# Moving one block's short convolution from VectorE to TensorE in a fused attention and long-convolution kernel

## The chip, the core and the metric

The kernel runs on one core of one Trainium2 chip. A core has five engines that run their own instruction streams and wait for one another through semaphores: TensorE (PE in the profile, with its weight loads as PEld), VectorE (DVE), ScalarE (ACT), GpSimd (POOL) and SyncE (SP), and 16 DMA engines that serve queues issued from SP, ACT and POOL. The metric is device time in microseconds (us); three runs of the kernel before gave 206.75, 206.83 and 206.92 us.

## What is computed

Two independent parts share the launch, and their outputs stand side by side in the result (2048 rows of 1152 bf16 values).

```python
# A: sliding, dilated local attention. S=2048, D=576, 32 heads of 18, window 8, dilation 2
qkv = x @ wqkv
logits[s, w] = q[s] . k[s - 2*w] * 18**-0.5        # -1e9 where s - 2*w < 0
o = softmax(logits over w) weighted sum of v[s - 2*w]
a = o @ wo

# B: gated long convolution, one channel at a time (D=576)
k_shift[t] = sum over j=0..3 of k[t - j] * shift_k[:, j]     # four taps per channel
kv = k_shift * v
y  = causal convolution of kv with ssm_k over 2048 steps, by a transform of length 4096
b  = q * (y + kv * ssm_D)
```

## The kernel before

**Tiling.** Sequence rows are cut into four blocks of 512. Part A projects q, k and v so that channels lie on the 128 partitions (jobs `q..`, `k..`, `v..`, for instance `k13a` and `k13b`, by `project`), multiplies shifted k by q on VectorE (`L..`, `pair_product`), sums over the 18 channels of a head on TensorE (`G..`, `pair_sum`), takes the softmax in four steps `sm0a` to `sm0d` for one half of the positions and `sm1a` to `sm1d` for the other, spreads the weights over partitions by DMA (`D0` to `D5`), weighs v on VectorE (`V..`), sums on TensorE (`A..`) and multiplies by `wo` (`O..`). Part B forms kv for block i by the four taps (`Ti`), folds it into a symmetric and an antisymmetric half (`Mi0`, `Mi1`), transforms it by cosine and sine tables on TensorE (`x..`), does the same with the filter (`F`, `K..`), multiplies spectra on VectorE (`p..`), sums them on TensorE (`z..`), goes back (`i..`, `b..`) and gates with q (`g..`).

**Order.** Nothing is scheduled by a compiler. The string `ORDER` lists the jobs; each one, when called, issues its instructions to every engine that it uses, and every engine runs its instructions in that order. A prime behind a job's name sets a variant inside it. `LHOMES`, `VHOMES`, `OHOMES` and `PHOMES` say which buffer a job's result goes to, so a job also waits until an older job has read that buffer. PSUM holds four slots of two banks; a job that multiplies on TensorE takes one or two (`banks`) and whoever empties it gives it back.

**Taps.** `taps(i)` (lines 511 to 536) runs on VectorE alone. `load_k` loads the block seven rows deep into `kj`, positions on partitions, so that a tap is a shift inside a partition; `skb` holds the tap weights on every partition, which `spread_taps` makes at the start. For blocks 1 to 3 there are two multiplications of 4608 elements for each partition (line 517), three additions of 2304 (line 520) and the multiplication with v (line 536). `mirror` then turns kv into its two halves with the constant `fold`.

**ScalarE's tables.** The sine tables are made early (line 382, job `S1` last). Job `Ex` (`exponential`, lines 658 to 660) then loads the table set that holds both the exponential and the logarithm; the softmax uses Exp at line 752, Ln at line 763 and Exp at line 764.

Of the kernel before, what the change touches and what calls it, by code (L numbers as in the profile page):

```python
# [17 lines left out]
PSUM = bass.MemoryType.PSUM  # L18

ORDER = """  # L20
    T0 k03a' T1 S1 k03b I1 k02a k02b Lk2 Lv2 I0 k00a' Lk3 Lv3 M01 X5 k00b q10a Ex q10b Lf3 T2 Lo3 q13a' q13b
    k10a k10b T3 k13a' Lf2 k13b q12a q12b N2 Lo2 k01a M10 k01b Lf1 M00 k11a k11b q11a M11 q11b Lf0 N3 Lw SV L001
    k12a M20 k12b x001 M21 x021 q24a x020 q24b x000 Lo1 k24a Fr Lo0 Z2 N1 RG3 k24b RG2 F3 RG0 F2 L000 K310 G000
    K311 K210 K211 L002 K313 G001 RG4 F1 G002 L003 G003 K302 L004 G004 K301 L010 K212 L011 K303 K213 K203 N0 F0
    L012 K200 K300 G010 L013 K201 K312 K202 RG1 G011 G012 K113 K103 G013 L014 G014 K112 K102 K101 L100 K100 K010
    K111 K110 sm0a K001 K013 sm0b v24a' L101 v24b L102 G100 L103 G101 K012 sm0c sm0d U3 U2 K000 K011 K003 G102
    K002 D0 D1 v11a v11b G103 L104 G104 ak00 M30 v12a' v12b ak02 v01a ak01 L110 G110 M31 L111 G111 v01b v00a'
    L112 G112 L113 Wl v00b G113 x031 U1 L114 G114 V04 v10a' v10b A04 sm1a sm1b v02a v02b v03a' sm1c v03b x201
    V10 V11 sm1d V12 A10 v13a' v13b D2 x330 x310 x301 V13 A11 V20 V21 x200 x331 x230 x010 x221 A20 x321 V22 x210
    x011 V23 D3 V34 ax02 x220 x030 x300 D4 A21 V40 V41 A34 D5 O000' x211 V42 x320 x231 x111 x131 Tx2 A40 V43  # L30
    x120 x101 ax00 x130 ax01 V50 x121 x311 O001 A41 V51 O100' p000 x100 x110 O010 A50 V52 z000 O011' V53 O101
    A51 Tk2 p010 z010 ax10 O020' O021 p020 z020 O110' ak10 i000 p200 i02880 Q0 p100 z100 p101 p110 p111 Q1 z101
    i02881 i001 p121 p120 O111 z110 p201 z111 z120 p210 z121 O120 p211 z200 z210 z211 p212 z212 z201 p202 z202
    Tx3 p220 Tk3 p221 O030' p222 O121 b0288 z220 p301 z221 O031' p302 b00 z222 p303 i200 i100 g0 Q2 p300 y300
    p312 i12880 i201 i101 i12881 z300 z301 z303 p310 p311 y310 O130 b10 b1288 p313 g1 Q3 p322 O131' z310 p320
    z311 p321 z313 i22880 i300 b20 y320 p323 i22881 i301 b2288 g2 z320 z321 z323 b30 i3384L g30 g3384
"""

LHOMES = (0, 1, 2, 0, 1, 2, 0, 1, 2, 0, 1, 2, 0, 1, 0, 1, 0, 1, 0, 1)
# [12 lines left out]
def kernel(  # L52
# [13 lines left out]
    nc = tc.nc  # L66
    Bsz, S, D = A_x.shape
# [6 lines left out]
    kf = B_k.flatten_outer_dims()  # L74
    vf = B_v.flatten_outer_dims()
# [14 lines left out]
    NBL, BL = 4, 512  # L90
# [3 lines left out]
    HD = 288  # L94
    HB = 4 * D
# [25 lines left out]
    def kv_of(i):  # L121
        return view(xw, HB * KVS[i], [[D, 4], [1, D]])
# [21 lines left out]
    sp1 = s1.enter_context(tc.tile_pool(name="s1", bufs=1, reuse_waits="tile"))  # L144
# [23 lines left out]
    Ks = main.tile([128, 12 * HB], BF16, name="Ks")  # L168
# [8 lines left out]
    kjs, vts = [], []  # L177
# [6 lines left out]
    def load_k(i):  # L184

        eng = nc.sync
        kj = sp1.tile([128, 7, D], BF16, name="kj", bufs=2)
        r0 = BL * i
        low = [(0, 64)]
        if i == 0:  # L190
            nc.gpsimd.memset(kj[0:1, 0:3, :], 0.0)
            nc.gpsimd.dma_start(kj[0:1, 3:7, :], kf[0:4, :].unsqueeze(0))
            low = [(1, 49), (49, 64)]
        for a, b in ((3, 7), (0, 3)) if i == 0 else ((0, 7),):
            for p0, p1 in low:
# [5 lines left out]
        kjs.append(kj)  # L201

    def load_v(i):
        vt = sp1.tile([128, 4, D], BF16, name="vt", bufs=2)
# [3 lines left out]
        vts.append(vt)  # L208

    def load_filter(m):  # L210

# [14 lines left out]
    ident = main.tile([128, 128], BF16, name="ident")  # L226
# [22 lines left out]
    flip = main.tile([128, 128], BF16, name="flip")  # L249
# [58 lines left out]
    def halves(ap):  # L308
        return ap.rearrange("p (h d) -> p h d", h=2)
# [197 lines left out]
    for n in range(2):  # L507
        job(f"I{n}", table_i, n)
    tt = nc.vector.tensor_tensor

    def taps(i):
# [23 lines left out]
            add(pair[1])  # L535
        tt(kv, kv, vt, ALU.mult)
# [599 lines left out]
```

## Time and profile before

| what | value |
|---|---|
| median of 3 runs | 206.83 us (206.75 to 206.92) |
| profiled execution, first to last instruction | 204.6 us, granted TensorE clock 0.994 |
| PE busy | 196.9 us (96%), 2074 matmuls |
| DVE busy | 192.3 us (94%), 146 instructions |
| ACT busy | 155.6 us (76%) |
| POOL busy | 60.8 us (30%) |
| DMA | 38.48 MB, mean 188 GB/s |

The profile states the execution's span of 204.6 us and no separate time for what lies around it; the median is 2.2 us above that span. A row that begins with a line number (L322) speaks of that line of the kernel. An arrow in a name points from what is read to what is written (`ps_proj<-xw`); the releaser behind a wait is the engine and line whose end ended it. The chain of work that ended last follows the program back from its last instruction, at each step to what released it. A matmul's record includes its way through the array, so records overlap, and the start of one to the start of the next says more than a record's length.

### The profile page before, as it was taken

Reading aid. Unit: us, or ns where it says so; the run is one execution under the profiler, and the core shown is the slowest. Engines: PE = TensorE matmul, PEld = TensorE weight load, DVE = VectorE, ACT = ScalarE, POOL = GpSimd, SP = SyncE. Lnnn points to the kernel's source line nnn. Section 1 sums busy time; section 2 is a strip of 40 time slices with the busy share of each in tenths; the row PEclk is TensorE's granted clock in tenths of the full one; section 3 lists DMA queues with packets and bytes.
Section 4 is the critical chain, followed back from the end, with each engine's and each line's share of the span. In section 5 each row is a group of like instructions: output and inputs, shape, how many; then the busy total and the mean of one; then the engine's idle time right before and its main releaser. Section 6 shows DMA issues by size and latency. Waiting matters only on the chain.

```text
span 204.6 us, 5004 instructions
## 1 busy us (share of the span) xinstructions
PE 196.9 (96%) x2074; PEld 109.9 (54%) x2074; DVE 192.3 (94%) x146; ACT 155.6 (76%) x223; POOL 60.8 (30%) x106
## 2 busy tenths in 40 slices
PE   7999999999989999999999999999999999999990
PEld 2543544334455646543245556776666767766660
DVE  7559999999999999999999999999999999899992
ACT  4788995678899999966578678886778767767760
POOL 8989500011348581400380000004090001030300
PEclk9999999999999999999999999999999999999997
DMA  6999899989509869999899990879989303944555
GB/s 197 280 293 306 175 289 373 214 177 281 169 3 146 111 82 185 167 180 222 157 235 216 248 244 34 141 183 334 186 227 233 100 28 122 227 130 145 153 182 150
DMA packets 34916, 38.48 MB, mean 188 GB/s; under 512 B 17523, under 2 KB 28911, under 8 KB 34894
## 3 DMA queue, kind: packets, MB, share of 16 engines
q1 hardware_dynamic: 26668, 24.29, 46.5%
q0 software_dynamic: 5760, 11.36, 29.5%
q10 hardware_dynamic: 2466, 2.51, 3.6%
q8 instruction: 16, 0.26, 0.5%
q14 instruction: 6, 0.05, 0.1%
HBM read 13.11 MB, written 4.72 MB: 87 GB/s over the span
## 4 chain that ended last, share of the span: by engine, by line
PE 88%; DMA 3%; ACT 2%; DVE 2%; issue 1%; SPq 1%; DVEq 0%
PE ps_proj L322 18%; PE ps_fx L682 8%; PE ps_wo L888 8%; PE ps_z L975 8%; PE ps_inv L1010 7%; PE ps_acc L824 7%; PE ps_fk L567 5%; PE ps_log L720 5%; DMA Ks<-in_A_x_dram 3%; PE ps_proj L333 3%; PE ps_proj L326 3%; PE ps_proj L439 3%; PE ps_fk L568 3%; PE ps_fold L545 2%; PE ps_wo L880 1%
## 5 line engine op out<-in xcount | busy, mean ns | idle before, releaser
L322 PE MATMUL ps_proj<-xw 128*128 128x512 bf16 x160 | 38.5, 380 | 0.0
L706 DVE TENSOR_TENSOR av<-qk 128x4096 bf16<-128x4096 bf16 (+1 forms) x16 | 31.7, 2014 | 0.1
L322 PEld LDWEIGHTS <-xw 128*128 128x128 bf16 x160 | 13.9, 98 | 19.4 <-issue 5.7
L988 ACT ACTIVATE av<-ps_z 128x768 bf16<-128x768 f32 x23 | 17.2, 811 | 6.5 <-PE ps_z L975 6.0
L517 DVE TENSOR_TENSOR tB<-kj,skb 128x4608 bf16<-128x4608 bf16 (+1 forms) x8 | 19.3, 2416 | 0.1
L950 DVE TENSOR_TENSOR qk<-xw,Ks 128x2304 bf16<-128x2304 bf16 x14 | 18.9, 1354 | 0.3 <-PE ps_z L975 0.3
L684 ACT ACTIVATE xw<-ps_fx 128x576 bf16<-128x576 f32 x32 | 18.6, 665 | 0.3 <-PE ps_fx L682 0.2
L618 ACT ACTIVATE Ks<-ps_fk 128x576 bf16<-128x576 f32 x32 | 18.6, 699 | 0.2 <-PE ps_fk L568 0.2
L355 ACT ACTIVATE qk<-ps_proj 128x1024 bf16<-128x1024 f32 x14 | 14.3, 1023 | 5.2 <-PE ps_proj L333 2.8
L888 PE MATMUL ps_wo<-qk 128*128 128x288 bf16 x128 | 17.9, 287 | 0.0
L626 POOL DMA_DIRECT2D Ks<-Ks x8 | 10.1, 1426 | 26.0 <-PE ps_back L1059 19.3
L682 PE MATMUL ps_fx<-xw,TB 128*128 128x288 bf16 x128 | 17.7, 287 | 0.0
L567 PE MATMUL ps_fk<-Ks,TB 128*128 128x384 bf16 x62 | 16.5, 327 | 0.1
L824 PE MATMUL ps_acc<-av,ident 64*64 64x512 bf16 x160 | 15.3, 378 | 0.0
L1010 PE MATMUL ps_inv<-av,TI 128*128 128x288 bf16 (+1 forms) x112 | 15.2, 292 | 0.0
L568 PE MATMUL ps_fk<-Ks,TB 128*128 128x192 bf16 x62 | 15.2, 246 | 0.0
L682 PEld LDWEIGHTS <-TB 128*128 128x128 bf16 x128 | 11.9, 98 | 5.9 <-issue 2.7
L888 PEld LDWEIGHTS <-qk 128*128 128x128 bf16 x128 | 11.7, 98 | 5.4 <-issue 2.7
L355 ACT ACTIVATE v<-ps_proj 128x1024 bf16<-128x1024 f32 x9 | 9.3, 1033 | 6.5 <-PE ps_proj L322 4.5
L813 DVE TENSOR_TENSOR av<-Ks,v 128x4096 bf16<-128x4096 bf16 x6 | 13.5, 2286 | 0.0
L827 ACT ACTIVATE qk<-ps_acc 128x1024 bf16<-128x1024 f32 x8 | 8.2, 1024 | 6.7 <-PE ps_acc L824 6.7
L1010 PEld LDWEIGHTS <-TI 128*128 128x128 bf16 x112 | 10.6, 98 | 4.2 <-issue 1.1
(195 smaller groups left out, 441.6 us busy)
## 6 DMA issues: line engine op xcount, KB each, us to landing
Ks<-Ks POOLq DMA_DIRECT2D x8, 576.0 KB, 7.8
TB<-av SPq DMA_DIRECT2D x12, 256.0 KB, 5.4
kj<-in_B_k_dram SPq DMA_DIRECT2D x6, 504.0 KB, 7.0
vt<-in_B_v_dram SPq DMA_DIRECT2D x8, 288.0 KB, 5.3
Ks<-av SPq DMA_DIRECT2D x8, 256.0 KB, 5.6
out_dram<-qk ACTq DMA_DIRECT2D x5, 288.0 KB, 3.7
Ks<-in_A_x_dram SPq DMA_DIRECT2D x2, 576.0 KB, 5.4
xw<-in_A_wqkv_dram SPq DMA_DIRECT2D x2, 576.0 KB, 6.2
```

The source lines that it names most:

```text
L322: nc.tensor.matmul(ps[:, jp, :], wq(kb, comp, 128 * ct, 128), xT(kb, 1024 * jj + 512 * jp, 512), **se)
L355: nc.scalar.activation(view(t, o + pad + 1024 * jj, [[512, 2], [1, 512]]), ps[:], ACT.Copy)
L517: tt(to, view(kj, row * D, [[D, n], [D, 4], [1, D]]), view(skb, row * D, [[D, n], [0, 4], [1, D]]), ALU.mult)
L567: nc.tensor.matmul(o[:, 0:2], w, rhs[:, 0:2], start=start, stop=stop)
L568: nc.tensor.matmul(o[:, 2], w, rhs[:, 2], start=start, stop=stop)
L618: nc.scalar.activation(view(Ks, k_at(m, cs ^ (m & 1)) + 96 * gi, [[768, 3], [384, 2], [1, 96]]), acc3(ps), ACT.Copy, scale=(PSG, MSG)[cs][ ...
L682: nc.tensor.matmul(ps[:, pm, 0:HD], TX[:, 2 * pm + c, 128 * gi:128 * gi + 128], kv[:, 2 * c + pm, HD * h:HD * h + HD], start=(c == 0), sto ...
L706: tt(view(P, at, [[step, 4], [256, nj], [1, 256]]), view(t, o + 256 * hh, [[0, 4], [512, nj], [1, 256]]), view(tk, ok + 2 + 8 * ug + 256 * ...
L824: nc.tensor.matmul(acc[64 * o:64 * o + 64, h, :], ident[64 * h:64 * h + 64, 64 * h:64 * h + 64], view(P[s], 256 * u, [[2048, 2], [1, 256]] ...
L888: nc.tensor.matmul(ps[:, r, 0:HD], oT(hh, j + 2 * r, t)[:, o:o + 128], wo[:, t // 2, t % 2, HD * h:HD * h + HD], start=(t == 0 and not fli ...
L950: tt(product_home(n), view(xw, HB * XG[i] + QTR * t, [[HB, 3], [1, QTR]]), view(Ks, k_at(j - i, 0) + QTR * t, [[HB, 3], [1, QTR]]), ALU.mult)
L1010: nc.tensor.matmul(ps[:, c, 0:n], TI[:, sl, pm, 128 * c:128 * c + 128], Yall(j % 2, pm, sl, slice(c0, c0 + n)), start=(pm == 0 and sl == 0 ...
```

## The change

Block 3, the fourth, no longer has its taps taken by VectorE. Its rows of k are loaded channel by channel with two transposing DMAs into space at the start of `Ks` (528 positions, 16 of them ahead of the block). For each 128 channels and each tap there is a 128 by 128 diagonal matrix with the tap's weights, 16 of them and four of 64 by 64 for the last 64 channels; VectorE makes them with two multiplications of `ident` by the weights, which two DMAs on ScalarE's queue bring in at the start as `taps_w`. On TensorE, 64 positions of transposed k (every fourth column) are the weights and the diagonal is the moving operand; four taps add up in PSUM, even and odd partition halves side by side. That makes three jobs: `T31` and `T30` with 64 matmuls each, and `T3t` with 32. VectorE multiplies each result by v, straight out of PSUM. Block 3's v is loaded to the place of kv, with the two halves on the lower and upper 64 partitions rather than interleaved, and `mirror` uses a second constant `fold_t` for it, made by GpSimd. Blocks 0 to 2 are as before.

The whole `ORDER` is new. VectorE's share of block 3, ahead of the first products of pairs (L590 is a small negation, L706 a product), before:

```order
L536 TENSOR_TENSOR xw<-xw,vt 128x2304
L517 TENSOR_TENSOR tB<-kj,skb 128x4608
L520 TENSOR_TENSOR xw<-tB 128x2304
L517 TENSOR_TENSOR tB<-kj,skb 128x4608
L520 TENSOR_TENSOR xw<-xw,tB 128x2304 x2
L536 TENSOR_TENSOR xw<-xw,vt 128x2304
L590 TENSOR_SCALAR Ks<-Ks 1x576 x2
L706 TENSOR_TENSOR av<-qk 128x4096
```

The same place on VectorE in the changed kernel, where L765 is the product of pairs, L578 and L589 the multiplication by v out of PSUM:

```order
L563 TENSOR_TENSOR xw<-xw,vt 128x2304
L765 TENSOR_TENSOR av<-qk 128x4096
L649 TENSOR_SCALAR Ks<-Ks 1x576 x2
L765 TENSOR_TENSOR av<-qk 128x4096
L765 TENSOR_TENSOR v<-qk 128x4x1024
L765 TENSOR_TENSOR av<-qk 128x4096
L765 TENSOR_TENSOR av<-qk 128x2048
L578 TENSOR_TENSOR xw<-ps_tap,xw 128x2x512
L765 TENSOR_TENSOR v<-qk 128x4x1024
L578 TENSOR_TENSOR xw<-ps_tap,xw 128x2x512
L589 TENSOR_TENSOR xw<-ps_tap,xw 128x4x64
L765 TENSOR_TENSOR av<-qk 128x4096
```

The six instructions of block 3's taps are gone, the products of pairs follow block 2 at once, and three multiplications out of PSUM stand among them.

Job `Ex` moved from behind `q10a` to the very end of `ORDER`. ScalarE around the first softmax, before (L752 is the exponential, L763 and L764 the logarithm and the exponential of the sum, L618 and L355 evictions of the filter's transform and of v's projection):

```order
L618 ACTIVATE Ks<-ps_fk 128x6x96 x9
L752 ACTIVATE av<-av 128x2048
L355 ACTIVATE v<-ps_proj 128x1024
L618 ACTIVATE Ks<-ps_fk 128x6x96
L763 ACTIVATE av<-ps_tot 128x256
L764 ACTIVATE av<-av 128x256
L618 ACTIVATE Ks<-ps_fk 128x6x96 x4
```

and in the changed kernel, where L811, L822 and L823 are those three and L677 and L377 those evictions:

```order
L677 ACTIVATE Ks<-ps_fk 128x6x96 x2
L811 ACT_TABLE_LOAD
L811 ACTIVATE av<-av 128x2048
L677 ACTIVATE Ks<-ps_fk 128x6x96
L377 ACTIVATE v<-ps_proj 128x1024
L822 ACT_TABLE_LOAD
L822 ACTIVATE av<-ps_tot 128x256
L823 ACT_TABLE_LOAD
L823 ACTIVATE av<-av 128x256
L677 ACTIVATE Ks<-ps_fk 128x6x96 x3
```

Three table loads stand inside the first softmax now; the second has two, ahead of its logarithm and ahead of its last exponential, and one more stands at the program's end with `Ex`. The one that stood at line 659 among the projections is gone.

The diff, cut to its core (the rest of `ORDER` is new in the same way):

```diff
 ORDER = """
-    T0 k03a' T1 S1 k03b I1 k02a k02b Lk2 Lv2 I0 k00a' Lk3 Lv3 M01 X5 k00b q10a Ex q10b Lf3 T2 Lo3 q13a' q13b
-    k10a k10b T3 k13a' Lf2 k13b q12a q12b N2 Lo2 k01a M10 k01b Lf1 M00 k11a k11b q11a M11 q11b Lf0 N3 Lw SV L001
...
+    k00a' T0 k01a k01b T1 k00b Lk2 k03a' M01 k02a X5 Lv2 k02b I0 k10a S1 Lw T2 q10a k10b SV q10b k24a k24b k11a
+    RG0 L000 Lf2 k03b N2 q11a Lf3 Lk3 k13a' N3 Lo2 k11b Lv3 Lf0 k13b Lo3 q11b M00 k12a k12b M11 q12a q12b RG3
+    L001 RG2 q13a' F3 q24a q24b Lf1 L002 q13b M21 G000 G001 Fr Lo0 L003 L004 RG4 Lo1 F2 T31 G002 G003 G004 RG1
+    L010 T30 T3t K313 L011 K311 M30 v03a' v03b K210 L012 N1 K312 G010 G011 K302 K300 K212 K203 N0 L013 L014 K202
...
+    z310 z311 z313 Q3 O131' p320 i300 b20 O121 y320 z320 p321 i301 p323 g2 z321 z323 b30 i3384L g30 g3384 Ex
 """
@@
+    taps_w = main.tile([128, 5, 4], BF16, name="taps_w")
+    nc.scalar.dma_start(taps_w[:, 0:4, :], B_shift_k[0:512, :].rearrange("(kb p) j -> p kb j", p=128))
+    nc.scalar.dma_start(taps_w[64:128, 4, :], B_shift_k[512:576, :])
@@
+        if i in TURNED:
+            t = view(Ks, 0, [[1, 5 * KT]]) if i == TURNED[0] else sp1.tile([128, 7, D], BF16, name="kj", bufs=2)
+            rows = kf[BL * i - 16:BL * i + BL]
+            eng.dma_start_transpose(view(t, 0, [[KT, 4], [1, KT]]), rows[:, 0:512])
+            eng.dma_start_transpose(view(t, 4 * KT, [[1, KT]]), rows[:, 448:576])
+            kjs[i] = t
+            return
@@
+    nc.vector.tensor_tensor(diag, ident[:].unsqueeze(1).unsqueeze(1).to_broadcast([128, 4, 4, 128]),
+                            taps_w[:, 0:4, :].unsqueeze(3).to_broadcast([128, 4, 4, 128]), ALU.mult)
+    nc.vector.tensor_tensor(diag_t, ident[64:128, 64:128].unsqueeze(1).to_broadcast([64, 4, 64]),
+                            taps_w[64:128, 4, :].unsqueeze(2).to_broadcast([64, 4, 64]), ALU.mult)
@@
+    def turned(i, kb, c, j, e):
+        return view(kjs[i], KT * kb + 16 + (259 - c if e else c) - j, [[4, 64]])
+
+    def taps_pe(i, h):
+        ps, slot = banks("ps_tap")
+        for c in range(2):
+            for kb in range(4):
+                for j in (3, 2, 1, 0):
+                    for e in range(2):
+                        nc.tensor.matmul(ps[64 * e:64 * e + 64, c, 128 * kb:128 * kb + 128],
+                                         turned(i, kb, 2 * h + c, j, e), diag[:, kb, j, :],
+                                         start=(j == 3), stop=(j == 0), tile_position=(0, 64 * e))
+        kv = kv_of(i)[:, 2 * h:2 * h + 2, 0:512]
+        tt(kv, ps[:], kv, ALU.mult)
+        slots.append(slot)
+
+    def taps_pe_tail(i):
+        ps, slot = banks("ps_tap")
+        for c in range(4):
+            for j in (3, 2, 1, 0):
+                for e in range(2):
+                    nc.tensor.matmul(ps[64 * e:64 * e + 64, 0, 64 * c:64 * c + 64], turned(i, 4, c, j, e)[64:128],
+                                     diag_t[:, j, :], start=(j == 3), stop=(j == 0), tile_position=(64, 64 * e))
+        kv = kv_of(i)[:, :, 512:576]
+        tt(kv, view(ps, 0, [[64, 4], [1, 64]]), kv, ALU.mult)
+        slots.append(slot)
```

More of the change, by code (lines that the diff above doesn't have):

```diff
@@ L26 @@
[L26 to L35, printed above, removed]
@@ L36 @@
-    z311 p321 z313 i22880 i300 b20 y320 p323 i22881 i301 b2288 g2 z320 z321 z323 b30 i3384L g30 g3384
+    k00a' T0 k01a k01b T1 k00b Lk2 k03a' M01 k02a X5 Lv2 k02b I0 k10a S1 Lw T2 q10a k10b SV q10b k24a k24b k11a
+    RG0 L000 Lf2 k03b N2 q11a Lf3 Lk3 k13a' N3 Lo2 k11b Lv3 Lf0 k13b Lo3 q11b M00 k12a k12b M11 q12a q12b RG3
+    L001 RG2 q13a' F3 q24a q24b Lf1 L002 q13b M21 G000 G001 Fr Lo0 L003 L004 RG4 Lo1 F2 T31 G002 G003 G004 RG1
+    L010 T30 T3t K313 L011 K311 M30 v03a' v03b K210 L012 N1 K312 G010 G011 K302 K300 K212 K203 N0 L013 L014 K202
@@ new lines @@
+    K310 G012 F1 L100 G013 G014 F0 K200 v00a' K201 K303 v00b G100 K211 K301 L101 sm0a sm0b G101 L102 K213 v02a
+    Z2 v02b L103 sm0c G102 L104 sm0d D1 K102 K003 G103 L110 K001 G104 K111 v01a L111 U3 K101 K113 K011 v01b G110
+    K002 K000 G111 K100 K110 K012 L112 K013 L113 G112 K112 L114 K010 K103 G113 v11a G114 D0 V11 V10 v11b M20
+    ak00 v24a' v24b sm1a M31 x010 A10 sm1b v10a' v10b V13 v12a' sm1c D2 x231 x200 x210 V04 sm1d ak01 A04 x230
+    v12b V12 x211 x221 x030 V20 D3 A11 v13a' v13b V21 x000 D4 x201 A20 x330 x311 x220 V22 V23 V34 Wl x020 M10
@@ new lines @@
+    ax00 A21 x310 Tx2 x321 ak02 A34 V41 x320 V40 O000' x011 x031 V42 x001 x021 ax02 x121 ax01 x110 A40 V43 D5
+    x101 x131 I1 O001 x120 O100' p000 A41 V50 x100 V51 x301 U2 x111 U1 Tk2 x130 V52 O101 A50 x331 z000 O110' V53
+    A51 p010 z010 x300 O010 ax10 p020 z020 p101 O111 O011' p111 i02880 Q0 i000 ak10 p100 z100 Tx3 p110 p120 z101
+    i02881 i001 z120 p121 z121 z110 z111 O020' p200 p210 p211 z200 p212 z210 z211 z212 Tk3 p201 i100 z201 p202
+    z202 i101 p222 b00 i12880 p220 p221 z220 p301 b0288 g0 z221 p302 z222 i12881 b10 p303 O030' i22880 b1288
@@ L37 @@
+    i200 i22881 O031' p300 O021 y300 p312 z300 z301 b2288 z303 Q1 g1 i201 p311 Q2 p310 y310 O120 p313 O130 p322
+    z310 z311 z313 Q3 O131' p320 i300 b20 O121 y320 z320 p321 i301 p323 g2 z321 z323 b30 i3384L g30 g3384 Ex
 """
@@ L176, in kTok @@
         return view(Ks, k_at(m, 2), [[D, 4], [1, D]])
-    kjs, vts = [], []
+    kjs, vts = {}, {}
+    TURNED = (3,)
+    KT = 16 + BL
+    diag = view(Ks, 3 * HB, [[512, 4], [128, 4], [1, 128]])
+    diag_t = view(Ks, 3 * HB + 2048, [[64, 4], [1, 64]])[64:128]
     def load_x(qtr):
@@ L200, in load_k @@
                                                     ap=[[4 * D, 64], [-D, b - a], [1, D]]))
-        kjs.append(kj)
+        kjs[i] = kj
     def load_v(i):
+        if i in TURNED:
+            nc.sync.dma_start(kv_of(i)[0:64], vf[BL * i:BL * i + 256, :].rearrange("(p c) d -> p c d", c=4))
+            nc.sync.dma_start(kv_of(i)[64:128], bass.AP(tensor=vf.tensor, offset=vf.offset + (BL * i + 256 + 3) * D,
+                                                        ap=[[4 * D, 64], [-D, 4], [1, D]]))
+            return
         vt = sp1.tile([128, 4, D], BF16, name="vt", bufs=2)
@@ L207, in load_v @@
                                               ap=[[4 * D, 64], [-D, 4], [1, D]]))
-        vts.append(vt)
+        vts[i] = vt
     def load_filter(m):
@@ L266 @@
                                 base=-127, channel_multiplier=1)
+    fold_t = main.tile([128, 128], BF16, name="fold_t")
+    for h in range(2):
+        nc.gpsimd.tensor_tensor(fold_t[:, 64 * h:64 * h + 64], ident[:, 0:64], flip[:, 0:64], (ALU.add, ALU.subtract)[h])
     flip2 = main.tile([128, 128], BF16, name="flip2")
@@ L544, in mirror @@
                 for e in range(2):
-                    nc.tensor.matmul(pss[pm][64 * e:64 * e + 64, h, 0:HD], fold[:, 64 * pm:64 * pm + 64],
+                    nc.tensor.matmul(pss[pm][64 * e:64 * e + 64, h, 0:HD], (fold_t if i in TURNED else fold)[:, 64 * pm:64 * pm + 64],
                                      kv[:, 2 * n + e, HD * h:HD * h + HD], start=True, stop=True, tile_position=(0, 64 * e))
@@ L551 @@
     for i in range(NBL):
-        job(f"T{i}", taps, i)
+        if i in TURNED:
+            for h in range(2):
+                job(f"T{i}{h}", taps_pe, i, h)
+            job(f"T{i}t", taps_pe_tail, i)
+        else:
+            job(f"T{i}", taps, i)
         for n in range(2):
```

3 lines of the change are left out of this document (removed).

## The prediction, made before the changed kernel ran

> **What bounds the kernel now.** I read the page's engine totals and its chain first.
>
> ```profile
> span 204.6 us, 5004 instructions
> PE 196.9 (96%) x2074; PEld 109.9 (54%) x2074; DVE 192.3 (94%) x146; ACT 155.6 (76%) x223; POOL 60.8 (30%) x106
> PE 88%; DMA 3%; ACT 2%; DVE 2%; issue 1%; SPq 1%; DVEq 0%
> ```
>
> TensorE and VectorE are both nearly always busy, but the chain that ended last runs through TensorE for 88% of the span and through VectorE for 2%. Busy TensorE records need not mean full speed, so the next view is the windows: TensorE from its wait for the second quarter of x (9.87) to its last matmul (199.9).
>
> ```profile
> 9.87:56.00 46.13, 46.13 (x315) 19.56 (x316) 42.91 (x28) 37.50 (x48) 16.11 (x38) 1.00 1.01 254
> 56.00:62.00 6.00, 5.25 (x44) 3.43 (x43) 6.00 (x4) 5.99 (x9) 2.97 (x5) 1.00 0.13 19
> 62.00:82.00 20.00, 20.00 (x195) 11.63 (x195) 19.86 (x16) 19.95 (x35) 12.18 (x13) 1.00 0.89 131
> 82.00:100.00 18.00, 18.00 (x159) 7.80 (x156) 18.00 (x12) 13.39 (x19) 2.30 (x2) 1.00 0.95 190
> 100.00:150.00 50.00, 50.00 (x596) 30.06 (x598) 49.74 (x31) 37.45 (x55) 9.84 (x13) 1.00 0.85 197
> 150.00:199.90 49.90, 49.23 (x736) 33.77 (x727) 47.96 (x39) 35.78 (x54) 8.83 (x12) 1.00 0.57 154
> ```
>
> The columns are the window, its length, then busy time of PE, PEld, DVE, ACT and POOL. TensorE lacks 0.75 us between 56 and 62 and 0.67 us in the last window, 1.4 us of 190. Its list of waits says the same, and VectorE's largest wait is its first data.
>
> ```profile
> PE ps_log L720 <- DVE av L706: 0.6, 1, 0.6
> PE ps_inv L1029 <- ACT av L988: 0.3, 1, 0.3
> PE ps_back L1038 <- ACT v L1031: 0.2, 1, 0.2
> PE ps_x L410 <- DMA Ks<-in_A_x_dram: 0.2, 1, 0.2
> PE ps_z L975 <- DVE Ks L950: 0.2, 1, 0.2
> DVE xw L517 <- DMA kj<-in_B_k_dram: 4.2, 1, 4.2
> 12.28 1.36 DVE L517 TENSOR_TENSOR xw<-kj,skb 128x2304 bf16<-128x2304 bf16 x1 [4.16 <-DMA kj<-in_B_k_dram]
> ```
>
> Then the pace of runs in the chain, to see whether "busy" hides waiting:
>
> ```profile
> 20.42 0.57 PE ps_ti L397 x16
> 25.62 0.25 PE ps_x L428 x8
> 29.10 3.56 PE ps_proj L322 x16
> 85.03 0.87 PE ps_tot L762 x8
> ```
>
> L322 moves 512 columns: 3.56/16 = 222 ns each, 2.3 columns in a ns. L762 moves 256: 109 ns each, 2.35 in a ns. Two different jobs, one of them amid ScalarE's and VectorE's busiest time, go at one pace for a column, so TensorE streams; it does not dawdle behind others. VectorE is full as well (42.91 + 6.00 + 19.86 + 18.00 + 49.74 + 47.96 = 184.5 of 190, and 2.4 of the missing 5.5 lie ahead of its first data at 12.28). The two are balanced, so work taken off VectorE gains no more than the waits for it, while work put on TensorE lengthens the kernel.
>
> **The change part by part.** *VectorE's taps of block 3 go.* Their rows:
>
> ```profile
> 44.36 2.55 DVE L517 TENSOR_TENSOR tB<-kj,skb 128x4608 bf16<-128x4608 bf16 x1
> 46.94 1.36 DVE L520 TENSOR_TENSOR xw<-tB 128x2304 bf16<-128x2304 bf16 x1
> 48.34 2.56 DVE L517 TENSOR_TENSOR tB<-kj,skb 128x4608 bf16<-128x4608 bf16 x1
> 50.93 2.75 DVE L520 TENSOR_TENSOR xw<-xw,tB 128x2304 bf16<-128x2304 bf16 x2
> 53.71 1.36 DVE L536 TENSOR_TENSOR xw<-xw,vt 128x2304 bf16<-128x2304 bf16 x1
> L1020 DVE TENSOR_TENSOR TB<-ps_back,TB 128x384 bf16<-128x384 f32 x2 | 1.0, 554 | 0.6 <-PE ps_back L1038 0.6
> L1020 DVE TENSOR_TENSOR TB<-ps_back,TB 128x768 bf16<-128x768 f32 x1 | 1.0, 954 | 0.0
> ```
>
> They sum to 10.6 us. Back come two multiplications of 1024 elements out of PSUM and one of 256. From 554 and 954 ns for 384 and 768 such elements, one element costs 1.04 ns, so 1024 take 1.22 and 256 take 0.42: 2.9 us. VectorE is relieved of 7.7 us.
>
> *The diagonals*, 2048 elements on 128 partitions and 256 on 64, both factors in SBUF, one repeated along the inner dimension. Low end: the softmax's subtraction, which also repeats an operand, takes 1.2 us for 2048 (L748, below). High end: the PSUM pace, about 2.3. With the small one, 1.4 to 2.7 us. VectorE waits 4.2 us for the first `kj` just there; that covers either, so I charge nothing. Without that cover it would be VectorE's time, not TensorE's.
>
> *TensorE's taps.* 128 matmuls of 64 weight columns by 128 moving ones, alternating between the array's column halves, each with its own weight load, and 32 by 64. No job of TensorE is dropped. The nearest row is L397: the same shape, the same alternation, own weights each: 0.57/16 = 36 ns. A floor comes from L762's pace: 128 columns take 54 ns, and with two halves at once 27 ns each. So the 128 cost 3.5 to 4.6 us. For the 32 the nearest row is L428 (same 64 wide weights, twice the moving columns), 31 ns: 1.0 at most, 0.5 at half. Together 4.0 to 5.6; long runs pay the change between jobs seldom, so I take 4.6.
>
> The Trainium skill, "TensorE: Matmul & The Clock Gate", section "Back-to-back issue gap", speaks against this change: it gives about 81 ns for each matmul in a stream of weight load and 128-column matmul. By it the 160 would cost an estimated 13.0 us; the trace's 36 ns for L397, which is such a stream, disagrees, and the sum keeps the row.
>
> *The start.* `taps_w` is 576 pieces of 8 bytes in two DMAs ahead of the first table load on ScalarE, while the second quarter of x, for which TensorE waits, is on its way.
>
> ```profile
> 3.12 6.70 DMA Ks<-in_A_x_dram
> q10 hardware_dynamic: 2466, 2.51, 3.6%
> ```
>
> ScalarE's queue shows 3.6% of 16 engines' 204.6 us for 2466 packets, 48 ns each at a kilobyte; 36 pieces on each engine are then at most 1.7 us, and zero if they slip between. Tiny pieces should cost well under a kilobyte's: 0.3.
>
> *Queues.* On SP, block 3's two transposing loads stand behind two of the four filter loads. Their data are wanted only at `T31`, some 50 us into the program, so nothing waits. The early `SV` job only lets the products start earlier.
>
> *Waits filled.* Of the five TensorE waits above, those for L706 (0.6) and L950 (0.2) should go when VectorE is ahead, and the 0.2 at other hand-overs: minus 1.0 at most, and I take all of it. The two ScalarE ones lie in the last job, which is unchanged.
>
> *New waits.* `M30` follows `T3t` on TensorE after two filter units only, and needs VectorE's two multiplications: 1.22 + 0.42 against about 1 us of cover: 0.3 with the semaphores. Bigger: with `Ex` at the end, ScalarE loads tables inside the softmaxes, three times in the first and twice between the second's sum and its result.
>
> ```profile
> L659 ACT ACT_TABLE_LOAD x1 | 1.3, 1283 | 0.0
> 86.36 0.42 ACT L764 ACTIVATE av<-av 128x256 bf16<-128x256 f32 x1
> 87.64 1.22 DVE L756 TENSOR_TENSOR av<-av 128x2048 bf16<-128x2048 bf16 x1
> L748 DVE TENSOR_TENSOR av<-av 128x2048 bf16<-128x2048 bf16 x1 | 1.2, 1225 | 0.0
> 108.58 2.28 DVE L813 TENSOR_TENSOR qk<-Ks,v 128x4096 bf16<-128x4096 bf16 x1
> 110.37 0.42 ACT L764 ACTIVATE xw<-xw 128x256 bf16<-128x256 f32 x1
> 110.82 1.23 DVE L756 TENSOR_TENSOR av<-av,xw 128x2048 bf16<-128x2048 bf16 x1
> ```
>
> VectorE's scaling L756 followed ScalarE's last exponential by 0.9 us in the first softmax and by nothing in the second. Three loads of 1.28 are 3.85, less 0.9: 3.0 late; two are 2.5 late. VectorE waits some 5.5 us of its 7.7, and behind L756 stand the next products of pairs and of v. For those TensorE's `G` and `A` jobs wait. Nothing arrives if VectorE is that far ahead, 5.5 if TensorE is right behind; VectorE is ahead by part of its relief, so I take 1.0. The load taken out at line 659 was not on the chain.
>
> The Trainium skill, "ScalarE: Activation LUTs", section "What ACT_TABLE_LOAD costs", adds about 1380 ns of draining to the 1283 of a load. By it the first softmax would be 7.1 us late and the second 5.3; here the single row shows no idle time ahead of the load (0.0), and what a load between two dependent activations costs no run here shows.
>
> **Sum.** On the profiled execution: 204.6 + 4.6 + 0.3 - 1.0 + 0.3 + 1.0 = 209.8 us of span. The 2.2 us between its span and the median of 206.83 stay, so the forecast is 206.83 + 5.2 = **212.0 us**. Its own bounds: +3.0 (cheap taps, no new waits) to +8, 209.8 to 214.8.
>
> **Rivals.**
> 1. *VectorE sets the end, and the kernel gets faster.* Place: the whole stretch from 12 us on. For it: VectorE hardly waits there, and TensorE's ends are modelled. It would save 7.7 less up to 5.5 lost at the softmaxes, 199.1 to 204.6, about 202. It decides only if TensorE's 190 us hide at least the 4.6 of the taps as waiting; against it stands the one pace of L322 and L762.
> 2. *Strided weights load slowly.* The taps' weight columns are four positions apart, L397's adjacent. The only strided read of this kind in the trace is ScalarE's regrouping L780, 1316 ns for 576 elements at a step of 9, against 665 for L684, which reads adjacent ones from PSUM. Twice the price for the taps: +4.6, 216.6 us.
>
> ```profile
> L780 ACT ACTIVATE xw<-Ks 128x576 bf16<-128x576 bf16 x5 | 6.6, 1316 | 0.0
> L684 ACT ACTIVATE xw<-ps_fx 128x576 bf16<-128x576 f32 x32 | 18.6, 665 | 0.3 <-PE ps_fx L682 0.2
> ```
>
> 3. *The softmax waits reach TensorE whole*: 5.5 instead of 1.0, 216.5 us. For it: TensorE follows VectorE closely (0.2 us waits for L950, none long).
> 4. *Weight loads one at a time*: one of 64 columns is recorded as 109 ns; 160 of them are 17.4, 12.8 above my 4.6: 224.8 us. L397 itself ran at 36 ns a matmul, hence hardly likely.
>
> ```profile
> L397 PEld LDWEIGHTS <-TB 128*64 128x64 bf16 x32 | 1.0, 109 | 0.7 <-issue 0.7
> ```
>
> 5. *The new order sheds more than it adds*: shorter changes between TensorE's jobs and no new waits, 206.5 to 209. The only named waits are 1.5 us, less than the cheapest taps, so this needs gains that no row shows.
>
> **How the numbers follow.** Forecast 69%, rival 3 10%, rival 2 8%, rival 5 6%, rival 1 5%, rival 4 2%. The range 209.0 to 215.8 holds the forecast and the milder half of rivals 2 and 3. What a measurement can tell from no change is about 0.2%, 0.4 us. Faster: rival 1 and no more, 5%. The same: half of rival 5, 3%. Slower: 92%.
>
> **What would show it.** Right: `ps_tap` runs of 64 matmuls in 1.8 to 2.3 us; TensorE busy in all windows from 10 us on and ending 4 to 6 us later; VectorE with waits of 2 to 3 us at both scalings, released by ScalarE, and others for `ps_tap`. Rival 2 shows as `ps_tap` runs of 4 us, rival 3 as TensorE waits for pair products or for v's. I am wrong if TensorE's last matmul ends before 201 us, which would mean that its records were elastic.

## Result and the profile after

The changed kernel takes **219.18 us** (218.04 to 219.81), the kernel before 206.88 beside it: ratio 1.060, 95% interval 1.056 to 1.064, 12.3 us slower. The forecast was 212.0 with a range up to 215.8: the sign is right, the size is not. The profiled execution has a span of 218.1 us. Its engine totals and the shares of its chain:

```profile
span 218.1 us, 5322 instructions
...
PE 205.7 (94%) x2221; PEld 114.7 (53%) x2234; DVE 188.7 (87%) x145; ACT 162.7 (75%) x228; POOL 78.3 (36%) x108
...
PE 86%; ACT 9%; issue 2%; DVE 1%; ACTq 0%; DVEq 0%
```

TensorE still sets the end, but ScalarE now has 9% of the chain where it had 2%. TensorE's last matmul started at 199.61 us before and starts at 213.24 now; the rest of the program behind it is as long as before. So all of the loss lies ahead of that matmul. Windows of the changed kernel (window, length, busy time of PE, PEld, DVE, ACT and POOL with the number of instructions, then the granted clock, the DMA share and GB/s):

```profile
80.00:92.00 12.00, 10.01 (x82) 4.85 (x82) 7.79 (x5) 11.79 (x15) 3.35 (x5) 1.00 0.76 131
...
108.00:123.00 15.00, 12.72 (x117) 7.46 (x118) 10.16 (x7) 12.61 (x17) 0.00 (x0) 0.89 0.63 128
```

The two softmaxes (80 to 92 and 108 to 123) stand out: TensorE lacks 2.0 and 2.3 us there, VectorE 4.2 and 4.8. ScalarE is full in the first (11.79 of 12.00) and busy for 12.61 of 15.00 in the second, where the clock was lowered too. TensorE's waits in the changed kernel (waiting tile and line, releaser, us in total, times, longest):

```profile
PE ps_acc L897 <- ACT xw L743: 1.6, 1, 1.6
...
PE ps_fk L626 <- ACT Ks L677: 1.1, 1, 1.1
...
PE ps_tot L821 <- ACT av L811: 0.8, 1, 0.8
PE ps_inv L1069 <- ACT av L1047: 0.6, 1, 0.6
...
PE ps_fx L741 <- ACT xw L822: 0.3, 1, 0.3
```

and VectorE's, which waits for both scalings (L815) as forecast:

```profile
DVE av L815 <- ACT xw L823: 2.7, 1, 2.7
...
DVE av L815 <- ACT av L823: 2.2, 1, 2.2
```

Four of these five TensorE waits (1.6 + 1.1 + 0.8 + 0.3 = 3.8 us) are in the softmaxes, and all are for ScalarE, none for VectorE's products. L677 and L743 are evictions of PSUM that have nothing to do with the softmax, and L822 empties the slot of the softmax's own sum. L821 is that sum on TensorE: it waits for the exponential itself (L811), which a load put off. ScalarE's instructions around the first softmax say why they are late (start, duration, line):

```profile
81.52 1.28 ACT L811 ACT_TABLE_LOAD   x1
82.81 1.91 ACT L811 ACTIVATE av<-av 128x2048 bf16<-128x2048 bf16 x1
84.63 0.63 ACT L677 ACTIVATE Ks<-ps_fk 128x576 bf16<-128x576 f32 x1
85.16 1.02 ACT L377 ACTIVATE v<-ps_proj 128x1024 bf16<-128x1024 f32 x1
86.19 1.28 ACT L822 ACT_TABLE_LOAD   x1
87.49 0.38 ACT L822 ACTIVATE av<-ps_tot 128x256 f32<-128x256 f32 x1
87.89 1.28 ACT L823 ACT_TABLE_LOAD   x1
89.19 0.42 ACT L823 ACTIVATE av<-av 128x256 bf16<-128x256 f32 x1
89.51 1.71 ACT L677 ACTIVATE Ks<-ps_fk 128x576 bf16<-128x576 f32 x3
```

ScalarE takes its instructions in order. From 86.19 to 89.51 it empties one slot only, that of the sum (L822): two loads and two short activations stand ahead, and three evictions then run one after another. TensorE has four PSUM slots and runs out of them (start, duration, and in brackets the wait and its releaser):

```profile
90.19 0.32 PE L626 MATMUL ps_fk<-Ks,TB 128*128 128x384 bf16 x1 [1.06 <-ACT Ks L677]
```

The Trainium skill, "ScalarE: Activation LUTs", section "What ACT_TABLE_LOAD costs", adds some 1380 ns of draining to a load. The trace disagrees for the load between L822 and L823, which needs L822's result: L822 ends at 87.49 + 0.38 = 87.87, the load starts at 87.89 and ends at 89.17, and L823 starts at 89.19.

The taps, from the chain of the changed kernel:

```profile
56.13 2.12 PE ps_tap L574 x64
...
59.66 2.13 PE ps_tap L574 x63
61.79 1.10 PE ps_tap L586 x30
```

Together they take 5.35 us, 33 ns for one of the 128 (4.6 in all were forecast; three of the 160 records are missing).

### The profile page after: what moved, and what is told of

The parts are those of the page before. It is cut to its first block, busy times and chain, and to the rows that moved or that the text cites. A ratio compares the mean times of both kernels' runs of the same rounds, so it can differ in the third digit from the quotient of the medians.

```text
span 218.1 us, 5322 instructions
## 1 busy us (share of the span) xinstructions
PE 205.7 (94%) x2221; PEld 114.7 (53%) x2234; DVE 188.7 (87%) x145; ACT 162.7 (75%) x228; POOL 78.3 (36%) x108
## 4 chain that ended last, share of the span: by engine, by line
PE 86%; ACT 9%; issue 2%; DVE 1%; ACTq 0%; DVEq 0%
PE ps_proj L344 15%; PE ps_wo L947 8%; PE ps_z L1034 8%; PE ps_inv L1069 7%; PE ps_acc L883 7%; PE ps_fx L741 6%; PE ps_fk L626 4%; PE ps_log L779 4%; PE ps_proj L461 3%; PE ps_proj L348 3%; PE ps_proj L355 2%; PE ps_rev L661 2%; PE ps_fk L627 2%; PE ps_tap L574 2%; PE ps_fold L599 2%
## 5 line engine op out<-in xcount | busy, mean ns | idle before, releaser
L344 PE MATMUL ps_proj<-xw 128*128 128x512 bf16 x148 | 37.9, 385 | 1.3 <-issue 1.0
L765 DVE TENSOR_TENSOR av<-qk 128x4096 bf16<-128x4096 bf16 (+1 forms) x16 | 31.7, 2019 | 6.0 <-ACT qk L377 3.3
L685 POOL DMA_DIRECT2D Ks<-Ks x8 | 12.1, 1633 | 27.6 <-DMA Ks<-Ks 23.1
L677 ACT ACTIVATE Ks<-ps_fk 128x576 bf16<-128x576 f32 x32 | 18.6, 658 | 3.7 <-PE ps_fk L627 3.5
L1047 ACT ACTIVATE av<-ps_z 128x768 bf16<-128x768 f32 x23 | 17.4, 817 | 4.1 <-PE ps_z L1034 4.1
L743 ACT ACTIVATE xw<-ps_fx 128x576 bf16<-128x576 f32 x32 | 18.9, 659 | 0.9 <-PE ps_fx L741 0.5
L377 ACT ACTIVATE qk<-ps_proj 128x1024 bf16<-128x1024 f32 x14 | 14.1, 1023 | 7.1 <-PE ps_proj L355 5.7
L741 PE MATMUL ps_fx<-xw,TB 128*128 128x288 bf16 x128 | 18.7, 291 | 0.3 <-ACT xw L822 0.3
L1009 DVE TENSOR_TENSOR qk<-xw,Ks 128x2304 bf16<-128x2304 bf16 x14 | 18.7, 1354 | 0.2
L685 POOL DMA_DIRECT2D xw<-xw x2 | 2.5, 1234 | 42.3 <-ACT xw L743 33.3
L1069 PE MATMUL ps_inv<-av,TI 128*128 128x288 bf16 (+1 forms) x112 | 16.2, 292 | 0.6 <-ACT av L1047 0.6
L544 DVE TENSOR_TENSOR tB<-kj,skb 128x4608 bf16<-128x4608 bf16 (+1 forms) x6 | 14.3, 2383 | 0.1
L666 POOL DMA_DIRECT2D Ks<-Ks x4 | 5.9, 1469 | 23.3 <-ACT Ks L664 23.3
```

The lines of the kernel that those rows point to most:

```text
L344: nc.tensor.matmul(ps[:, jp, :], wq(kb, comp, 128 * ct, 128), xT(kb, 1024 * jj + 512 * jp, 512), **se)
L677: nc.scalar.activation(view(Ks, k_at(m, cs ^ (m & 1)) + 96 * gi, [[768, 3], [384, 2], [1, 96]]), acc3(ps), ACT.Copy, scale=(PSG, MSG)[cs][ ...
L741: nc.tensor.matmul(ps[:, pm, 0:HD], TX[:, 2 * pm + c, 128 * gi:128 * gi + 128], kv[:, 2 * c + pm, HD * h:HD * h + HD], start=(c == 0), sto ...
L743: nc.scalar.activation(view(xw, HB * XG[i] + 96 * gi + 1152 * h, [[HB, 2], [384, 3], [1, 96]]), view(ps, 0, [[512, 2], [96, 3], [1, 96]]), ...
L765: tt(view(P, at, [[step, 4], [256, nj], [1, 256]]), view(t, o + 256 * hh, [[0, 4], [512, nj], [1, 256]]), view(tk, ok + 2 + 8 * ug + 256 * ...
L1009: tt(product_home(n), view(xw, HB * XG[i] + QTR * t, [[HB, 3], [1, QTR]]), view(Ks, k_at(j - i, 0) + QTR * t, [[HB, 3], [1, QTR]]), ALU.mult)
```

## Experiments

Ratios are to the kernel before, run on the same chip beside it (206.1 to 206.4 us); differences in us are differences of ratios times 206.1.

**1. Ex early in the changed kernel.**

```diff
-    ... I0 k10a S1 Lw T2 ...  ... i3384L g30 g3384 Ex
+    ... I0 k10a S1 Ex Lw T2 ...  ... i3384L g30 g3384
```

> The changed kernel (219.2 us) with one edit: the job Ex, which loads one table for exponential and logarithm, goes from the end of the order to right behind S1, so that no table is loaded inside the softmaxes. Theory A (the five loads inside the softmaxes hold up ScalarE's evictions queued behind them, TensorE runs out of PSUM slots, and its clock drops after the pause): TensorE's pauses in the two softmaxes are 2.0 and 2.3 us and the clock at 0.89 costs some 1.65, so about 6 us go: 213.2, between 212 and 215; granted clock 1.00 in every window. Theory B (the size in the prediction: the loads reach TensorE with 1.0 us only, the rest of the loss is the taps and the new order): 218.2. Theory C (the loads are hidden altogether): 219.2.

Measured: 214.30 us, ratio 1.0386 (1.0364 to 1.0407): 4.3 us less than the changed kernel. Its two softmax windows:

```profile
80.00:92.00 12.00, 11.89 (x99) 6.08 (x98) 10.89 (x7) 10.63 (x16) 3.80 (x6) 1.00 1.00 172
108.00:123.00 15.00, 14.63 (x143) 8.32 (x138) 13.61 (x8) 11.90 (x17) 0.00 (x0) 1.00 0.80 171
```

TensorE's pauses are gone and so is the lowered clock. Theory A holds, with 4.3 us where it said about 6. But 8.0 of the 12.3 us are left, and the forecast's other terms make only 4.2 of them.

**2. Ex late in the kernel before.**

```diff
-    ... k00b q10a Ex q10b ...  ... g30 g3384
+    ... k00b q10a q10b ...  ... g30 g3384 Ex
```

> The kernel before (206.9 us) with one edit: Ex goes from behind q10a to the end of the order, so that its softmaxes load tables as the changed kernel's do. Theory A: ScalarE's queue holds up TensorE as in the changed kernel, 4 to 6 us: 211 to 213, with TensorE waiting for ScalarE in the two softmaxes. Theory B: 1.0 us, 207.9. Theory C: 206.9. If it costs far less here than Ex early gains in the changed kernel, the price belongs to where the new order puts evictions of PSUM behind the loads.

Measured: 213.79 us, ratio 1.0365 (1.0341 to 1.0389), 7.5 us slower: more than every theory. Its TensorE waits, VectorE's waits, and windows of TensorE's clock around a pause (the eighth number is the granted clock):

```profile
PE ps_acc L824 <- DVE av L813: 1.4, 1, 1.4
...
PE ps_fk L567 <- ACT Ks L618: 1.1, 1, 1.1
PE ps_fk L567 <- ACT av L763: 1.0, 1, 1.0
PE ps_tot L762 <- ACT av L752: 1.0, 1, 1.0
PE ps_fk L567 <- ACT Ks L605: 0.8, 1, 0.8
```
```profile
DVE av L756 <- ACT av L764: 3.4, 1, 3.4
...
DVE av L756 <- ACT xw L764: 2.0, 1, 2.0
```
```profile
92.20:94.60 2.40, 2.18 (x8) 1.04 (x7) 2.37 (x5) 1.23 (x3) 0.00 (x0) 0.50 0.17 22
...
95.00:95.40 0.40, 0.40 (x4) 0.10 (x1) 0.09 (x1) 0.00 (x0) 0.00 (x0) 1.00 0.27 41
```

VectorE's scaling waits 3.4 + 2.0 = 5.4 us, what the prediction worked out for it (5.5). Four of the TensorE waits are in the softmaxes, 4.5 us together. The fifth, for L605, is at 61 us and stands in place of the 0.6 for L706 that the kernel before has at 60, so it adds 0.2 at most. For some 3.4 us TensorE has half its clock, which is about 1.7 more: 6.4 of the 7.5, and the rest is open. One of the four (L824 for VectorE's L813, 1.4 us) is the path that the prediction had in mind, the other three are for ScalarE. That the same loads cost 3.2 us less in the changed kernel may come from VectorE's relief or from another set of neighbours; no run parts the two.

**3. One tap of four, in the new order.** Experiment 1 with this edit besides:

```diff
-                for j in (3, 2, 1, 0):        (twice)
+                for j in (0,):
-    start=(j == 3), stop=(j == 0)
+    start=True, stop=True
```

> The kernel with Ex early, and of the four taps of block 3 on TensorE only the first is computed (j = 0, 40 matmuls instead of 160); this leaves out three quarters of that filter, everything else stays. If TensorE sets the end and a tap costs 33 ns, as the runs of 64 and 63 matmuls in the changed kernel's chain show, 120 of them are 4.0 us: 4.0 below the kernel with Ex early. If the taps lie in time that TensorE would otherwise wait (VectorE or ScalarE sets the end): 0 to 1 us below.

Measured: 213.36 us, ratio 1.0346 (1.0318 to 1.0373): only 0.8 us below experiment 1. The three runs of tap matmuls last 1.6 us instead of 5.35, so 3.7 were taken off TensorE (4.0 were expected). TensorE has a new wait:

```profile
PE ps_fold L599 <- DVE xw L578: 1.8, 1, 1.8
```

`M30` follows `T3t` after two filter units and needs VectorE's multiplications. The second of them starts at 62.30 us in experiment 1 and at 61.38 here: VectorE, which has a product of pairs in between, is only 0.9 us earlier. With all four taps (experiment 1) it ends at 63.53 and TensorE comes to `M30` at 64.37, so nothing waits. The wait explains 1.8 of the 2.9 us that did not arrive. The profiled execution's span is 1.5 us shorter than that of experiment 1 (211.2 and 212.7); the rest stays open. Two of the four executions had a mean clock of 0.985 and 0.987, against 0.993 in the other two, and took 0.9 us more; no trace of those is at hand.

**4. The old order with the taps on TensorE.**

```diff
-    (new ORDER)
+    (ORDER of before, without T3, and ahead of K310:)  F2 L000 T31 T30 T3t K310
```

> The changed kernel's code with the order of the kernel before; T3 is taken out and T31 T30 T3t stand ahead of K310, Ex stays where it was before. It has the taps on TensorE and nothing of the new order. If TensorE sets the end: 206.9 + 5.35 for the taps as traced - 1.0 at most for refilled waits, and up to 0.6 for the two multiplications that free the slots: 211.3 to 212.9. If the new order alone (beside Ex) costs something, this one lies below the kernel with Ex early by that much; if the two agree, the new order is free apart from Ex. If VectorE's relief gains: 206.9 or less.

Measured: 211.26 us, ratio 1.0244 (1.0218 to 1.0271), 5.0 us slower than before. That is the whole price of the taps, all parts together, within the expected range (4.4 to 6.0 above before) and near the forecast of the prediction for everything (5.2). The new order, Ex apart, costs the difference to experiment 1: 2.9 us. VectorE had time to spare here, which it spent waiting for a DMA:

```profile
DVE Ks L649 <- DMA Ks<-Ks: 7.6, 1, 7.6
```

Where are the 2.9 us? TensorE's waits and the clock show little of them: experiment 1 has one new wait, 0.6 us for L1047. I compared the start of each matmul with the start of the next in both traces. A matmul behind one that uses as many rows and columns of the array starts on time; behind one of another shape (128 rows by 128 columns, 64 by 128, 128 by 64, 128 by 32, 64 by 64) it starts some 95 to 105 ns late, whatever the two lines are. In the records there are 136 such changes in the kernel before, 139 in experiment 4, and 164 in experiment 1 and in the changed kernel. 25 more at 95 ns are 2.4 us. With the wait of 0.6 that makes 3.0 us, the size of the difference of the medians. In the two profiled executions TensorE's last matmuls are 3.7 us apart (204.13 and 207.84), so some of it may have another cause. A job with a tail of 64 rows has a prime in `ORDER` that says whether the tail comes first, so that neighbours can share a shape; the new order has as many primes, but more neighbours that do not fit.

**5. More changes of shape, in the kernel before.**

```diff
-    k00a' ... q13a' ... k13a' ... v11a ... v12a' ... v00a' ... v02a ... v13a' ... O000' ... O001 ... O100' ...
+    k00a  ... q13a  ... k13a  ... v11a' ... v12a ... v00a  ... v02a' ... v13a ... O000  ... O001' ... O100 ...
     (and the primes of O010, O011, O020, O110, O111 and O030)
```

> The kernel before (206.1 us in the runs beside the last four) with the apostrophes of 17 jobs in its order turned over: whether a job does its 64-row tail before or after its 128-row body. Same matmuls, same jobs, same places; only neighbours no longer share a shape of the array (rows and columns used), so that TensorE changes shape 28 times more, as many more as the changed kernel does against the kernel before. Theory D (in the traces a matmul behind one of another shape starts 95 ns later than one behind its own shape, and this is what the new order costs beside Ex): 28 x 0.095 = 2.7 us, 208.8, between 208.2 and 209.3. Theory E (the gap is only how matmul ends are modelled in the records, or other things in the new order cost its 3.0 us): 206.1, within 0.4.

Measured: 209.73 us, ratio 1.0173 (1.0137 to 1.0208): 3.6 us slower (2.8 to 4.3) by nothing but primes, 136 changes turned into 164. Theory E falls and Theory D holds in kind, though the median lies above its range of 208.2 to 209.3. Not all of it is the changes themselves: TensorE has another wait for ScalarE, the one that experiment 2 has too,

```profile
PE ps_fk L567 <- ACT Ks L605: 0.8, 1, 0.8
```

and its wait of 0.6 for L706 is gone. 28 changes at 95 ns with these two make 2.9 us, and the profiled execution's last matmul is 2.8 us later than in the kernel before. Two of the four executions had a mean clock of 0.992 and 0.993, against 0.998, and took 1.1 us more, which lifts the median; no trace of those is at hand. The chain shows the price of a change at one line:

```profile
100.37 0.97 PE ps_proj L322 x4
101.34 0.32 PE ps_proj L333 x2
...
110.82 0.86 PE ps_proj L322 x4
111.68 0.37 PE ps_fx L682 x3
```

Four matmuls of L322 take 0.86 us when L682 with its 128 rows follows, and 0.97 when L333 with 64 rows follows.

The Trainium skill, "TensorEngine Tiling (Array Packing)", section "Key Properties", says that a change of the tiling mode drains TensorE. The trace fits that, with a delay of some 0.1 us at each change.

**6. Fewer changes, in the kernel before.** Primes set at `k01a`, `k11a` and `k12a`.

> The kernel before with the apostrophe set at three jobs, k01a, k11a and k12a, so that TensorE changes shape 4 times less. Theory D: 4 x 0.095 = 0.38 us less, 205.8. Theory E: no difference.

Measured: 206.22 us, ratio 0.9988 (0.9970 to 1.0006). The expected 0.9982 is inside, and so is no difference: undecided, and no version that surely beats the kernel before.

**7. VectorE relieved, TensorE given nothing.**

```diff
     def taps(i):
+        if i == 3:
+            tt(kv_of(3), view(kjs[3], 0, [[D, 4], [1, D]]), vts[3], ALU.mult)
+            return
```

> The kernel before, with the filter of block 3 left out on VectorE and put nowhere: of its five operations (10.6 us) only the last multiplication stays (1.4 us), so VectorE is relieved of 9.2 us and TensorE gets nothing. The output lacks that filter. If TensorE sets the end, as predicted, only its waits for VectorE can go, 1.0 us at most: 205.1 to 206.1. If VectorE sets the end (rival 1 of the prediction), up to 9.2 go: 197 to 199.

Measured: 206.75 us, ratio 1.0007 (0.9989 to 1.0026). VectorE is 8.5 us less busy and nothing comes of it, not even the 1.0 us of waits. Its totals, VectorE's new waits and TensorE's:

```profile
PE 197.6 (96%) x2074; PEld 110.4 (54%) x2074; DVE 183.8 (90%) x141; ACT 155.5 (76%) x223; POOL 64.2 (31%) x106
```
```profile
DVE av L709 <- PE ps_log L723: 3.5, 1, 3.5
...
DVE Ks L593 <- DMA Ks<-Ks: 3.1, 1, 3.1
```
```profile
PE ps_fk L570 <- ACT Ks L608: 0.7, 1, 0.7
```

TensorE's wait of 0.6 for VectorE's L706 (L709 here) is gone; one of 0.7 for ScalarE stands in its place.

**8. One tap of four, in the old order.** The edit of experiment 3 on the kernel of experiment 4.

> The changed kernel's code in the order before (211.3 us), and of block 3's four taps only the first: 40 matmuls instead of 160, three quarters of that filter left out. In the new order the same cut took off only 0.9 of the 4.0 us that the 120 matmuls last, since M30 stands right behind T3t and TensorE then waited 1.8 us for VectorE's multiplication. Here M30 stands some 40 us later. If that is the reason: 4.0 less, 207.3. If the tap matmuls run in time that TensorE does not need in any order: about 1 less, 210.3.

Measured: 209.44 us, ratio 1.0160 (1.0124 to 1.0196): 1.7 us below experiment 4, not 4.0. So the hand-over to `M30` explains experiment 3 only in part. Here TensorE runs into others, as its waits show:

```profile
PE ps_tap L586 <- ACT Ks L664: 1.0, 1, 1.0
PE ps_z L1034 <- DVE av L1009: 0.4, 1, 0.4
```

1.0 us for a PSUM slot, 0.4 for a product, and smaller gaps at line 1034. TensorE is the bound, but ScalarE and VectorE follow it within a microsecond: what is added to it costs nearly in full (5.0 us in experiment 4), what is taken away gains less than half.

**9. One load instead of five.**

```diff
-    ... L101 sm0a sm0b G101 ...  ... g30 g3384 Ex
+    ... L101 sm0a Ex sm0b G101 ...  ... g30 g3384
```

> The changed kernel (1.0597 of the kernel before) with Ex directly ahead of sm0b, the first exponential: one table load of 1.28 us at the place of the first of the five, and none of the other four. With Ex far ahead it was 1.0386 of before. Theory A (each load stands in ScalarE's queue ahead of evictions that TensorE needs, and the pauses of TensorE and its halved clock come from the two loads between the sum's eviction and the scaling): the single load costs at most its own 1.28 us: ratio 1.039 to 1.045, 214.3 to 215.6 against 206.2. Theory F (any load at the start of the softmax brings the pause and the clock loss): 1.050 to 1.060.

Measured: 215.22 us, ratio 1.0437 (1.0410 to 1.0464), 1.05 us (0.3 to 1.8) above experiment 1. ScalarE's row of the load, which stands where the first of the five did, and TensorE's one new wait, which is for the exponential behind the load:

```profile
81.36 1.28 ACT L718 ACT_TABLE_LOAD   x1
```
```profile
PE ps_tot L821 <- ACT av L811: 0.9, 1, 0.9
```

So the first load costs most of its own length; if the prices add up, the other four cost the remaining 3.3 us of 4.3. The time is within Theory A's range and below Theory F's. But its path is another than Theory A says: TensorE's sum waits for the exponential itself, and not for an eviction behind the load.

**10. Ex early and fewer changes, in the new order.** Experiment 1 with the primes of k00a, k10a, k11a, v00a, v10a, O001 and O100 turned over.

> The changed kernel with Ex early (1.0386 of before) and the apostrophes of seven jobs turned over (k00a, k10a, k11a, v00a, v10a, O001, O100), so that TensorE changes shape 8 times less; nothing else moves. Theory D, 95 to 120 ns for a change: 0.76 to 0.96 us less, a ratio of 1.034 to 1.035. Theory E (changes of shape cost nothing in the new order, something else does): 1.0386 again.

Measured: 213.34 us, ratio 1.0344 (1.0318 to 1.0370), 0.9 us less than experiment 1 and inside Theory D's 1.034 to 1.035. The records have 157 changes, 7 fewer rather than 8. The two intervals touch, so this is support only; experiment 5 is the stronger evidence, in the order of the kernel before. That the 2.9 us of the new order are mostly changes of shape rests on the count and on these two.

## Why the prediction was right in its sign and short in its size

The 12.3 us are the taps 5.0 (experiment 4), the rest of the new order 2.9 (experiment 1 less experiment 4) and the table loads 4.3 (the changed kernel less experiment 1). Each is the step from one kernel to the next, so they add up by construction, and they are not independent: in the order of the kernel before, the loads alone cost 7.5 (experiment 2). Against the forecast's terms, the loads missed by 3.3 us, the new order by 2.9 and all the rest by 0.8. Of the signs that the prediction named, the tap runs (2.12 us) and VectorE's waits at both scalings (2.2 and 2.7) came; TensorE was not busy in all windows, and its last matmul is 13.6 us later instead of 4 to 6.

- **What bounds the kernel.** Right. VectorE's relief gains nothing (experiment 7), and rival 1 falls. The sentence that it gains no more than the waits for it was even generous: the term "minus 1.0 at most, and I take all of it" should have been nothing.
- **Taps on TensorE, 4.6 within 4.0 to 5.6.** Right: 5.35 traced, 5.0 in time. L397 was the right row for the 128 (33 against 36 ns). The 32 of the tail have half the columns and were to take 1.0 at most, and they take 1.10 us, some 35 ns each. Rivals 2 and 4 fall. The Trainium skill, "TensorE: Matmul & The Clock Gate", section "Back-to-back issue gap", gives about 81 ns for each matmul; the trace, with 33, disagrees.
- **Diagonals at nothing, start 0.3.** Right for the diagonals: VectorE made them from 8.34 to 11.2 us, and its first taps began at 11.28 instead of 12.28. The start costs about 0.1: TensorE's first matmul on the second quarter of x is at 10.00 instead of 9.87.
- **Hand-over `T3t` to `M30`, 0.3.** Not there as long as all taps are computed; experiment 3 shows that it costs 1.8 when TensorE comes earlier.
- **"Nothing arrives if VectorE is that far ahead, 5.5 if TensorE is right behind; ... I take 1.0."** This is the first step that failed: 4.3 us in place of 1.0, nearly half of the miss of 7. The delay of VectorE was sized well (2.2 and 2.7 us in the changed kernel, 5.4 in experiment 2). The path was wrong. The prediction followed the loads to VectorE's scaling, and through its products to TensorE; it did not ask what else stands in ScalarE's own queue. Evictions of the filter, of v and of x stood behind the loads, and TensorE waited for slots (1.6 + 1.1 + 0.3 us); and the softmax's sum on TensorE waited for the exponential behind the first load (0.8 us). VectorE's slack cannot help with either. Rival 3 had a price nearer the truth (5.5), but by VectorE's products, for which TensorE waits nowhere in the softmaxes of the changed kernel.
- **The pause's second price.** In the profiled execution the clock fell to half for some 3.4 us after TensorE's pause at 116 to 118, about 1.7 us (windows of the changed kernel):

```profile
116.00:118.00 2.00, 0.38 (x7) 0.18 (x9) 0.61 (x1) 1.99 (x4) 0.00 (x0) 1.00 0.00 0
...
118.80:119.20 0.40, 0.40 (x12) 0.17 (x4) 0.28 (x1) 0.17 (x1) 0.00 (x0) 0.50 0.16 41
...
122.00:122.40 0.40, 0.40 (x5) 0.33 (x4) 0.40 (x1) 0.27 (x1) 0.00 (x0) 1.00 0.97 154
```

  The execution of 218.04 us had a mean granted clock of 1.000, the one of 218.56 one of 0.995 and those of 219.8 one of 0.991. So the pause's price seems to come in some executions only and to make the spread of the changed kernel; only the profiled execution, one of the slower two, has a trace.
- **The new order at nothing but its waits.** The second step that failed: 2.9 us. The prediction named "shorter changes between TensorE's jobs" as a hope (rival 5) and did not count them, though the order of both kernels was known. Counted, 25 more changes of shape than in experiment 4, at 95 ns, are 2.4 us. Most of the rest is the wait of 0.6 for L1047 at 178, where VectorE's product L1009 comes late; from the chain of the changed kernel:

```profile
176.04 1.37 DVE Ks L1009
...
178.02 0.82 ACT av L1047
```

## What to carry to other kernels

When an instruction with a latency of its own (a table load) moves into a stage, price it in the queue where it stands: list what comes behind it on that engine, and who needs that, before following its own result. Before a new order is costed at nothing, count how often neighbours on TensorE differ in rows and columns: each change was some 95 ns here, and a kernel with 28 more of them was 2.8 to 4.3 us slower. In this kernel, where all engines are nearly full, work added to the bounding engine cost its length, while work removed, from it or from its neighbour, gained less than half of that or nothing.

## What was not expected of the hardware

The price of a change of shape on TensorE is the first; it hides in records that overlap, and shows when starts are compared. The second is GpSimd. In the kernel before, its small selections ran in VectorE's pause ahead of the first taps; in the changed kernel they run beside VectorE's taps. The same statement before (L280) and after (L302):

```profile
9.39 0.21 POOL L280 TENSOR_SCALAR_AFFINE_SELECT E<-E 128x32 bf16<-128x32 bf16 x1
```
```profile
14.26 1.22 POOL L302 TENSOR_SCALAR_AFFINE_SELECT E<-E 128x32 bf16<-128x32 bf16 x1
...
15.71 2.42 POOL L302 TENSOR_SCALAR_AFFINE_SELECT E<-E 128x32 bf16<-128x32 bf16 x1
```

0.21 us became 1.2 to 2.4, about the length of one of VectorE's instructions at that place (1.4 to 2.6), and GpSimd's setup ended at 41 us instead of 23. No run tests whether VectorE is the cause. Nobody waited for it: no wait of another engine names GpSimd.
